# Routed attention and a mixture of experts on one core: similarities and router logits computed transposed, in column tiles of 32

## The chip, the cores and the metric

One core of one Trainium2 chip. The metric is the device time of one execution in microseconds, as the median of the runs shown; lower is better.

## The reference

Attention over 4 batch elements, 8 heads, 768 tokens and a head size of 64, in which a query sees only the keys of its own cluster; then a layer of 8 experts of which each token takes one.

```
q_assign = argmax(einsum('bhsd,hcd->bhsc', q_n, c_n))     # 16 centroids per head
k_assign = argmax(einsum('bhsd,hcd->bhsc', k_n, c_n))
mask     = q_assign[:, :, :, None] == k_assign[:, :, None, :]
attn     = softmax(where(mask, q @ k.T / 8, -1e9))
x        = (attn @ v)  ->  (3072 tokens, 512)
logits   = x @ w_gate                                     # 8 experts
e, gate  = argmax(logits), softmax(logits)[argmax]
out      = gate * (relu(x @ w1[e]) @ w2[e])               # 512 -> 1024 -> 512
```

All inputs and outputs are fp32. An argmax takes the first of equal values.

## The kernel before

The work has three stages. The first is attention with the router's logits. Two heads of one batch element make a group; there are 16 groups, four for each batch element. The rows of q and k are turned by the tensor engine (`turn`, three pieces), so that `qk[g]` has the 2 x 64 components of two heads on the partitions and the tokens along the free dimension. `similar(g)` multiplies each block of 128 tokens, as the stationary operand, with the 32 centroids of the two heads (`cblk`, block diagonal), for q and k: 12 matmuls, whose result already has the tokens on the partitions. `assign` and `assign2` make a one-hot row of each token's cluster on VectorE and GpSimd (`ohs`), `put(g, 0)` for q and `put(g, 1)` for k turn the one-hot rows to `ohT`. A masked score is then a second matmul of `ohT` added on top of the first of `qk`, and the exponential of ScalarE (`A`) makes the masked ones zero. `score(u)` does this for one block of 128 keys against 384 queries of both heads, `attend(u)` multiplies with v two blocks later (the two heads in two column tiles of 64), `T` adds up the denominators on VectorE, and `finish(g, half)` sums them over the partitions, takes the reciprocal on VectorE and writes the normalized half into `XT[b, hp]`.

When the four groups of a batch element are done, `x_turn(b, j)` turns `XT` back into rows, `logits` multiplies each block of 128 tokens of `XT`, stationary, with `wg` (8 columns), accumulated over four blocks of 128 components, `gate` makes the gate's value, and `keep_rows` writes the rows to a DRAM buffer.

The order is written out by hand. One group has 12 units u; the loop takes two units at a time, and one such iteration issues the two scores, two attends, and then the jobs that `at(u, ...)` placed at these units. The jobs of a group g lie around the units of the group before it (LEAD = 14, LAG = 2). Counted from the first unit of the group before: turn at -2 to 0, finish of the last group's second half at 2, similar at 2, assign at 3, assign2 at 5, put 0 at 7, finish of this group's first half at 8, put 1 at 8. For a batch element, counted the same way in the group that follows it, x_turn stands at 3 to 8, logits at 4 and 6, gate at 8, keep_rows at 9.

PSUM has three pools: two tiles of two banks for scores, two for the attended sums, and `ps_m`, two tiles named `mps`, for everything else: turn, similar, put, finish, x_turn and logits take turns in these two. A tile is free when the instruction that reads it out is done; which of the two a job gets is fixed when the kernel is built.

The second stage is the routing: from the logits `lg` VectorE works out for each token its expert and its place in the expert's list, and matmuls scatter the token numbers into index tables. The third stage gathers the rows of each expert by indirect DMA, runs the two layers, and scatters the results. Its weights are loaded three experts ahead. The function `in_general` is a way out for inputs that would overflow and doesn't run here.

Of the kernel before, what the change touches and what calls it, by code (L numbers as in the profile page):

```python
# [8 lines left out]
F32 = mybir.dt.float32  # L9
# [4 lines left out]
ALU = mybir.AluOpType  # L14
# [168 lines left out]
def kernel(  # L183
# [11 lines left out]
    nc = tc.nc  # L195
    B, H, S, D = q.shape
    C = centroids.shape[1]
    P = 128
    NQ = S // P
    HP = H // 2  # L200
    NG = B * HP
    HS = S // 2
    G = 4 * NQ
    N = B * S
    Dm = H * D
    E = moe_w_gate.shape[1]
    F = moe_w1.shape[2]
    DB = Dm // P
    FB = F // P
    NT = N // P  # L210
    KA = D + C
    XW = Dm + 4
    assert D == 64 and H * C == P and NQ * P == S and DB * P == Dm and FB * P == F

    NJ = N // E // P
    CAP = NJ * P
# [6 lines left out]
    consts = ctx.enter_context(tc.tile_pool(name="consts", bufs=1))  # L223
# [3 lines left out]
    def fetch(e):  # L227
        w1 = wpool.tile([P, DB, F], F32, name="w1")
        w2 = wpool.tile([P, FB, Dm], F32, name="w2")
        nc.sync.dma_start(out=w1, in_=moe_w1[bass.ds(e, 1)].rearrange("e (a p) f -> p (e a) f", p=P))  # L230
        nc.sync.dma_start(out=w2, in_=moe_w2[bass.ds(e, 1)].rearrange("e (a p) d -> p (e a) d", p=P))
        return w1, w2
# [3 lines left out]
    ident = consts.tile([P, P], F32)  # L236
    ident_b = consts.tile([P, P], BF16)

    def iota(name, shape, pattern, base, mult):
        ti = consts.tile(shape, I32, name=name + "_i")  # L240
        tf = consts.tile(shape, F32, name=name)
        nc.gpsimd.iota(ti, pattern=pattern, base=base, channel_multiplier=mult)
        nc.gpsimd.tensor_copy(tf, ti)
        return tf

    lg = rte.tile([P, NT, E], F32)
# [6 lines left out]
    with ExitStack() as actx:  # L253
# [3 lines left out]
        asg = actx.enter_context(tc.tile_pool(name="asg", bufs=2))  # L257
        ap = actx.enter_context(tc.tile_pool(name="ap", bufs=4))
        tp_ = actx.enter_context(tc.tile_pool(name="tsum", bufs=2))
        stat = actx.enter_context(tc.tile_pool(name="stat", bufs=2))  # L260
# [4 lines left out]
        ps_m = actx.enter_context(tc.tile_pool(name="ps_m", bufs=2, space=PSUM))  # L265
# [4 lines left out]
        def load(g):  # L270
            b, hp = divmod(g, HP)
            for name, src in (("q", q), ("k", k)):
                t = rows[g, name] = ld.tile([P, NQ, 2, D], F32, name=name + "_in")
                for a in range(2):
                    nc.sync.dma_start(out=t[:, :, a, :], in_=src[b, 2 * hp + a].rearrange("(p j) d -> p j d", j=NQ))
            t = rows[g, "v"] = ld.tile([P, 2, NQ, D], F32, name="v_in", bufs=3)
            nc.sync.dma_start(
                out=t.rearrange("p a j d -> p a (j d)"),
                in_=v[b, 2 * hp : 2 * hp + 2].rearrange("a (p j) d -> p a (j d)", j=NQ),
            )  # L280

        csb = consts.tile([P, D], F32)
        nc.scalar.dma_start(out=csb, in_=centroids.rearrange("h c d -> (h c) d"))
        wg = consts.tile([P, DB, E], F32)
        nc.scalar.dma_start(out=wg, in_=moe_w_gate.rearrange("(a p) e -> p a e", p=P))
        load(0)
        load(1)
        make_identity(nc, ident)
# [1 line left out]
        first_c = iota("first_c", [P, C], [[-1, C]], C, 0)  # L290
        first_e = iota("first_e", [P, E], [[-1, E]], E, 0)
        ones_h = consts.tile([P, D], F32)
        nc.gpsimd.memset(ones_h, 1.0)
        nc.gpsimd.memset(rsum, 0.0)
        nc.gpsimd.memset(rlow, 0.0)

        ohs = []
        for i in range(2):
            t = consts.tile([P, 2 * NQ, 2, D], BF16, name=f"oh{i}")
# [23 lines left out]
        cblk = consts.tile([P, HP, 2, C], F32)  # L323
# [6 lines left out]
        qk, sims, ohT = {}, {}, {}  # L330
# [20 lines left out]
                nc.scalar.copy(dst, src)  # L351

        def similar(g):
            ps = ps_m.tile([P, 512], F32, name="mps")
            for w in range(2):
                for j in range(NQ):
                    c0 = (w * NQ + j) * 2 * C
                    nc.tensor.matmul(  # L358
                        ps[:, c0 : c0 + 2 * C], lhsT=qk[g][:, w, j * P : (j + 1) * P],
                        rhs=cblk[:, g % HP].rearrange("p a c -> p (a c)"), start=True, stop=True,  # L360
                    )
            sims[g] = asg.tile([P, G, C], F32, name="sim")
            nc.scalar.copy(sims[g], ps[:, 0 : G * C].rearrange("p (t c) -> p t c", c=C))

        def assign(g):

            sim = sims.pop(g)
            mx = asg.tile([P, G], F32, name="mx")
            nc.vector.tensor_reduce(mx, sim, axis=AX, op=ALU.max)
            rank = asg.tile([P, G, C], F32, name="rank")  # L370
            nc.vector.tensor_tensor(rank, sim, mx.unsqueeze(2).to_broadcast([P, G, C]), op=ALU.is_ge)
            nc.gpsimd.tensor_tensor(rank, rank, first_c[:, None, :].to_broadcast([P, G, C]), op=ALU.mult)
            sims[g] = rank

        def assign2(g):
            rank = sims.pop(g)
# [7 lines left out]
        def put(g, w):  # L384
            if w == 0:
                ohT[g] = ohp.tile([P, 2, S], BF16, name="ohT")
            ps = ps_m.tile([P, 512], F32, name="mps").bitcast(BF16)
            for j in range(NQ):
                nc.tensor.transpose(
                    ps[:, j * P : (j + 1) * P], ohs[g % 2][:, w * NQ + j].rearrange("p a c -> p (a c)"), ident_b  # L390
                )
            if w == 0:
                nc.scalar.copy(ohT[g][:, 0, :], ps[:, 0:S])
            else:
                nc.vector.tensor_scalar(
                    ohT[g][:, 1, :], ps[:, 0:S], scalar1=BIG, scalar2=-BIG, op0=ALU.mult, op1=ALU.add
                )
# [3 lines left out]
        X, XT = {}, {}  # L401
# [63 lines left out]
                nc.tensor.transpose(ps[:, c * P : (c + 1) * P], XT[b, c][:, j * P : (j + 1) * P], ident)  # L465
            nc.scalar.copy(X[b][:, j, 0:Dm], ps)

        def logits(b, js):
            ps = ps_m.tile([P, 512], F32, name="mps")
            for i, j in enumerate(js):  # L470
                for c in range(DB):
                    nc.tensor.matmul(
                        ps[:, i * E : (i + 1) * E], lhsT=XT[b, c][:, j * P : (j + 1) * P], rhs=wg[:, c, :],
                        start=(c == 0), stop=(c == DB - 1),
                    )
            nc.vector.tensor_copy(
                lg[:, b * NQ + js[0] : b * NQ + js[-1] + 1, :],
                ps[:, 0 : len(js) * E].rearrange("p (j e) -> p j e", e=E),
            )

        def gate(b):
            ts = slice(b * NQ, (b + 1) * NQ)
# [19 lines left out]
        def at(u, f, *a):  # L502
            jobs.setdefault(u, []).append((f, a))
# [3 lines left out]
        for g in range(NG):  # L507
            u0 = g * UG - LEAD
            for piece in range(3):
                at(u0 + piece, turn, g, piece)  # L510
            at(u0 + 4, similar, g)
            at(u0 + 5, assign, g)
            at(u0 + 7, assign2, g)
            at(u0 + 9, put, g, 0)
            at(u0 + 10, put, g, 1)
            for half in range(2):
                at(g * UG + (half + 1) * NQ + LAG, finish, g, half)
        for g in range(2, NG):
            at((g - 2) * UG + LAG + 2, load, g)
        for b in range(B):  # L520
            u0 = (b + 1) * HP * UG + LAG + 1
            for j in range(NQ):
                at(u0 + j, x_turn, b, j)
            at(u0 + 1, logits, b, (0, 1, 2))
            at(u0 + 3, logits, b, (3, 4, 5))
            at(u0 + 5, gate, b)
            at(u0 + 6, keep_rows, b)

        def early(e):
# [40 lines left out]
    with tc.tile_pool(name="sm", bufs=1) as sm, tc.tile_pool(name="rps", bufs=1, space=PSUM) as rps:  # L570
# [23 lines left out]
            op=ALU.is_gt,  # L594
# [11 lines left out]
            op=ALU.is_le,  # L606
# [75 lines left out]
    mps = mctx.enter_context(tc.tile_pool(name="moe_ps", bufs=3, space=PSUM))  # L682
# [77 lines left out]
    with tc.If(nx > XU):  # L760
        with tc.For_i(XU, nx, 1) as i:
# [4 lines left out]
            g = dict(n=1, w=fetch(ex), gi=lambda j: gi[:, 0:1], si=lambda j: gi[:, 1:2], apart=False)  # L766
# [35 lines left out]
```

## Time and profile before

| | us |
|---|---|
| median of 3 runs | 1006.79 |
| lowest, highest run | 993.57, 1011.89 |
| profiled execution, its own time | 1008.31 |
| its span, first to last instruction | 1006.5 |
| attention stage, from the first score to the last attend | 20.3 to 499 |
| tail of the logits and routing, to the first matmul of the experts | 499 to 547.6 |
| experts | 547.6 to 1006.5 |

The mean granted clock of the tensor engine over the span is 0.934 of full speed (2.4 GHz); it has two levels, 1.00 and 0.50 (1.2 GHz), and a mean between them says how long each held.

An fp32 matmul stands in the trace as two passes, each with its own weight load; so 12 matmuls of `similar` are 24 rows of MATMUL and 24 of LDWEIGHTS. PE is the matmul, PEld the weight load. Matmul ends are modelled, so the length of a block is better read from the start of one block to the start of the next. The bracket at the end of a timeline row is the idle time of that engine before it and what released it.

### The profile page before, as it was taken

How to read it: one execution, taken by the hardware profiler on the slowest of the kernel's cores; microseconds unless marked ns; L12 is line 12 of the kernel's file. 1: busy time of each engine (PE TensorE's matmuls, PEld its weight loads, DVE VectorE, ACT ScalarE, POOL GpSimd, SP SyncE). 2: the span in 40 equal slices, each digit the busy share in tenths (PEclk: the TensorE clock that was granted, in tenths of full speed). 3: DMA queues.
4: the chain of work that ended last, by engine and by line, in shares of the span. 5: the costliest groups of instructions: out<-in, count | busy, mean ns of one | idle time of the engine just before them, and what ended most of it. 6: DMA issues, size and time to landing. Idle time of an engine off the chain costs nothing. (4 is left out here: it accounts for less than half of the span.)

```text
span 1006.5 us, 11290 instructions
## 1 busy us (share of the span) xinstructions
PE 941.5 (94%) x4655; PEld 525.4 (52%) x4655; DVE 386.2 (38%) x493; ACT 257.1 (26%) x392; POOL 210.8 (21%) x218
## 2 busy tenths in 40 slices
PE   5999999999999999999967999999999999988896
PEld 4555555454555555555365555545455454555664
DVE  2677745677447775477752101011010100000110
ACT  4444434444334443344410010101100010010100
POOL 3133321333113332132323020101201011010100
PEclk8999989999789998899955999999999999998998
DMA  7016223161221612100012242324334233446610
GB/s 166 16 41 214 49 48 109 32 199 35 48 80 32 215 48 48 73 7 1 1 63 64 83 145 97 133 105 160 141 128 146 100 131 125 159 165 223 236 62 9
DMA packets 82587, 99.02 MB, mean 98 GB/s; under 512 B 52959, under 2 KB 57055, under 8 KB 82016
## 3 DMA queue, kind: packets, MB, share of 16 engines
q1 hardware_dynamic: 76480, 77.60, 24.9%
q0 software_dynamic: 5376, 20.56, 5.2%
q8 instruction: 39, 0.64, 0.3%
q14 instruction: 20, 0.16, 0.1%
q10 hardware_dynamic: 672, 0.05, 0.0%
HBM read 85.57 MB, written 14.20 MB: 99 GB/s over the span
## 5 line engine op out<-in xcount | busy, mean ns | idle before, releaser
L706 PE MATMUL hp<-xgT,w 128*128 128x384 f32 (+1 forms) x896 | 212.9, 399 | 0.8 <-DVE xgT L698 0.8
L719 PE MATMUL zp<-w,h_sb 128*128 128x512 f32 x480 | 211.2, 599 | 0.0
L419 ACT ACTIVATE A<-sps 128x768 f32<-128x768 f32 x192 | 155.2, 811 | 110.9 <-PE sps L417 106.7
L414 PE MATMUL sps<-qk 64*128 64x384 f32 x768 | 183.1, 557 | 0.4 <-ACT A L419 0.4
L706 PEld LDWEIGHTS hp<-xgT,w 128*128 128x128 f32 x896 | 142.4, 193 | 74.2 <-issue 8.6
L426 DVE TENSOR_TENSOR T<-T,A 128x768 f32<-128x768 f32 x128 | 133.9, 1046 | 88.8 <-ACT A L419 82.7
L711 DVE TENSOR_SCALAR h_sb<-hp 128x384 f32<-128x384 f32 (+1 forms) x56 | 24.8, 444 | 359.2 <-PE hp L706 359.2
L434 PE MATMUL O<-A,v_in 128*64 128x384 f32 x768 | 149.7, 512 | 0.0
L719 PEld LDWEIGHTS zp<-w,h_sb 128*128 128x128 f32 x480 | 91.4, 193 | 109.8 <-issue 109.8
L725 POOL DMA_INDIRECT out_dram<-zo,s_idx x30 | 30.1, 1002 | 391.5 <-ACT zo L724 378.5
L454 POOL TENSOR_TENSOR rsum<-rsum,rd 128x384 f32<-128x384 f32 x32 | 32.0, 1000 | 333.0 <-DVE rd L450 333.0
L434 PEld LDWEIGHTS O<-A,v_in 128*64 128x64 f32 x768 | 48.4, 141 | 89.0 <-issue 88.9
L414 PEld LDWEIGHTS sps<-qk 64*128 64x128 f32 x768 | 69.6, 203 | 46.9 <-issue 25.6
L450 DVE RECIPROCAL rd<-mps 128x384 f32<-128x384 f32 x32 | 81.8, 2557 | 3.2 <-PE mps L446 2.1
L724 ACT ACTIVATE zo<-zp,xg 128x512 f32<-128x512 f32 x30 | 20.6, 687 | 222.1 <-PE zp L719 222.1
L713 ACT ACTIVATE h_sb<-hp 128x384 f32<-128x384 f32 (+1 forms) x56 | 22.3, 399 | 214.8 <-PE hp L706 214.8
L417 PE MATMUL sps<-ohT 64*128 64x384 bf16 x384 | 69.0, 352 | 0.0
L358 PEld LDWEIGHTS mps<-cblk,qk 128*128 128x128 f32 x384 | 44.3, 193 | 9.2 <-issue 9.2
L455 POOL TENSOR_SCALAR rd<-rd 128x384 f32<-128x384 f32 x32 | 45.9, 1433 | 2.8
L422 DVE SCALAR_TENSOR_TENSOR T<-A 128x768 f32<-128x768 f32 x32 | 31.2, 976 | 39.6 <-ACT A L419 39.6
L358 PE MATMUL mps<-cblk,qk 128*128 128x32 f32 x384 | 46.0, 278 | 0.0
L697 PE MATMUL tp<-ident,xg 128*128 128x128 f32 x120 | 19.3, 298 | 21.2 <-DMA xg<-x_rows,g_idx 18.8
(140 smaller groups left out, 556.0 us busy)
## 6 DMA issues: line engine op xcount, KB each, us to landing
w<-in_moe_w_dram SPq DMA_DIRECT2D x28, 2048.0 KB, 9.4
x_rows<-x POOLq DMA_DIRECT2D x4, 1548.0 KB, 5.5
q_in<-in_q_dram SPq DMA_DIRECT2D x32, 192.0 KB, 4.4
k_in<-in_k_dram SPq DMA_DIRECT2D x32, 192.0 KB, 4.7
v_in<-in_v_dram SPq DMA_DIRECT2D x16, 384.0 KB, 3.3
xg<-x_rows,g_idx POOLq DMA_INDIRECT x30, 6.9
out_dram<-zo,s_idx POOLq DMA_INDIRECT x30, 2.7
csb<-in_centroids_dram ACTq DMA_DIRECT2D x1, 32.0 KB, 1.9
```

The lines of the kernel that those rows point to most:

```text
L358: nc.tensor.matmul(ps[:, c0 : c0 + 2 * C], lhsT=qk[g][:, w, j * P : (j + 1) * P], rhs=cblk[:, g % HP].rearrange("p a c -> p (a c)"), start ...
L414: nc.tensor.matmul(ps[:, a, 0:HS], lhsT=qk[g][r, 1, ks], rhs=qk[g][r, 0, qs], start=True, stop=False)
L417: nc.tensor.matmul(ps[:, a, 0:HS], lhsT=ohT[g][r, 1, ks], rhs=ohT[g][r, 0, qs], start=False, stop=True)
L419: nc.scalar.activation(A[u], ps[:, :, 0:HS], AF.Exp)
L422: nc.vector.scalar_tensor_tensor(T[g, half], in0=A[u - 1], scalar=1e-9 / P, in1=A[u], op0=ALU.add, op1=ALU.add)
L426: nc.vector.tensor_tensor(T[g, half], T[g, half], A[u], op=ALU.add)
L434: nc.tensor.matmul(O[g, half][a * D : (a + 1) * D, 0:HS], lhsT=rows[g, "v"][:, a, j, :], rhs=a_[:, a, :], start=(j == 0), stop=(j == NQ - 1),)
L450: nc.vector.reciprocal(rd, ps[:, 0:HS])
L454: nc.gpsimd.tensor_tensor(rsum, rsum, rd, op=ALU.add)
L455: nc.gpsimd.tensor_scalar(rd, rd, scalar1=1e-30, scalar2=None, op0=ALU.is_lt)
L706: nc.tensor.matmul(hp[:, :cols], lhsT=g["w"][0][:, c, fb * P : (fb + 1) * P], rhs=g["xT"][:, c, :cols], start=(c == 0), stop=(c == DB - 1),)
L719: nc.tensor.matmul(zp, lhsT=g["h"][:, fb, j * P : (j + 1) * P], rhs=g["w"][1][:, fb, :], start=(fb == 0), stop=(fb == FB - 1),)
```

## The change

`similar` makes the centroids the stationary operand, 32 columns, and moves the tokens: four matmuls (q and k, two halves of 384 tokens each), each into its own 32 partitions of one PSUM tile, that is into its own column tile of the array. The result `simT` is copied by ScalarE and has the centroids on the partitions. A new step `similar2`, two units later, turns it by three transposes into the form that `assign` wants, with a second copy by ScalarE; the order of the token blocks in it is another, which `put` undoes by its index. `assign` works in place.

`logits` does the same with `wg`, padded from 8 to 32 columns (GpSimd clears it and copies the 8 columns in), in three column tiles of 256 tokens for a whole batch element at once; `logits2` turns the result by two transposes and VectorE copies it into `lg`.

The order changes with it: similar2 at 4, assign at 5 (before 3), assign2 at 6 (5), put 0 at 8 (7), put 1 at 9 (8); logits at 3, one block in place of two at 4 and 6, logits2 at 5, gate at 7 (8).

```diff
--- before.py
+++ after.py
@@ -210,7 +210,7 @@
     NT = N // P
     KA = D + C
     XW = Dm + 4
-    assert D == 64 and H * C == P and NQ * P == S and DB * P == Dm and FB * P == F
+    assert D == 64 and C == 16 and H * C == P and NQ % 2 == 0 and NQ * P == S and DB * P == Dm and FB * P == F
 
     NJ = N // E // P
     CAP = NJ * P
@@ -281,8 +281,8 @@
 
         csb = consts.tile([P, D], F32)
         nc.scalar.dma_start(out=csb, in_=centroids.rearrange("h c d -> (h c) d"))
-        wg = consts.tile([P, DB, E], F32)
-        nc.scalar.dma_start(out=wg, in_=moe_w_gate.rearrange("(a p) e -> p a e", p=P))
+        wg_in = consts.tile([P, DB, E], F32)
+        nc.scalar.dma_start(out=wg_in, in_=moe_w_gate.rearrange("(a p) e -> p a e", p=P))
         load(0)
         load(1)
         make_identity(nc, ident)
@@ -291,6 +291,9 @@
         first_e = iota("first_e", [P, E], [[-1, E]], E, 0)
         ones_h = consts.tile([P, D], F32)
         nc.gpsimd.memset(ones_h, 1.0)
+        wg = consts.tile([P, DB, 32], F32)
+        nc.gpsimd.memset(wg, 0.0)
+        nc.gpsimd.tensor_copy(wg[:, :, 0:E], wg_in)
         nc.gpsimd.memset(rsum, 0.0)
         nc.gpsimd.memset(rlow, 0.0)
 
@@ -351,26 +354,33 @@
                 nc.scalar.copy(dst, src)
 
         def similar(g):
+
             ps = ps_m.tile([P, 512], F32, name="mps")
-            for w in range(2):
-                for j in range(NQ):
-                    c0 = (w * NQ + j) * 2 * C
-                    nc.tensor.matmul(
-                        ps[:, c0 : c0 + 2 * C], lhsT=qk[g][:, w, j * P : (j + 1) * P],
-                        rhs=cblk[:, g % HP].rearrange("p a c -> p (a c)"), start=True, stop=True,
-                    )
+            for t in range(4):
+                w, half = divmod(t, 2)
+                nc.tensor.matmul(
+                    ps[t * 2 * C : (t + 1) * 2 * C, 0:HS], lhsT=cblk[:, g % HP].rearrange("p a c -> p (a c)"),
+                    rhs=qk[g][:, w, half * HS : (half + 1) * HS], start=True, stop=True,
+                )
+            sims[g] = asg.tile([P, HS], F32, name="simT", bufs=1)
+            nc.scalar.copy(sims[g], ps[:, 0:HS])
+
+        def similar2(g):
+            simT = sims.pop(g)
+            ps = ps_m.tile([P, 512], F32, name="mps")
+            for i in range(NQ // 2):
+                nc.tensor.transpose(ps[:, i * P : (i + 1) * P], simT[:, i * P : (i + 1) * P], ident)
             sims[g] = asg.tile([P, G, C], F32, name="sim")
-            nc.scalar.copy(sims[g], ps[:, 0 : G * C].rearrange("p (t c) -> p t c", c=C))
+            nc.scalar.copy(sims[g], ps[:, 0:HS].rearrange("p (t c) -> p t c", c=C))
 
         def assign(g):
 
             sim = sims.pop(g)
             mx = asg.tile([P, G], F32, name="mx")
             nc.vector.tensor_reduce(mx, sim, axis=AX, op=ALU.max)
-            rank = asg.tile([P, G, C], F32, name="rank")
-            nc.vector.tensor_tensor(rank, sim, mx.unsqueeze(2).to_broadcast([P, G, C]), op=ALU.is_ge)
-            nc.gpsimd.tensor_tensor(rank, rank, first_c[:, None, :].to_broadcast([P, G, C]), op=ALU.mult)
-            sims[g] = rank
+            nc.vector.tensor_tensor(sim, sim, mx.unsqueeze(2).to_broadcast([P, G, C]), op=ALU.is_ge)
+            nc.gpsimd.tensor_tensor(sim, sim, first_c[:, None, :].to_broadcast([P, G, C]), op=ALU.mult)
+            sims[g] = sim
 
         def assign2(g):
             rank = sims.pop(g)
@@ -387,7 +397,7 @@
             ps = ps_m.tile([P, 512], F32, name="mps").bitcast(BF16)
             for j in range(NQ):
                 nc.tensor.transpose(
-                    ps[:, j * P : (j + 1) * P], ohs[g % 2][:, w * NQ + j].rearrange("p a c -> p (a c)"), ident_b
+                    ps[:, j * P : (j + 1) * P], ohs[g % 2][:, (j % (NQ // 2)) * 4 + w * 2 + j // (NQ // 2)].rearrange("p a c -> p (a c)"), ident_b
                 )
             if w == 0:
                 nc.scalar.copy(ohT[g][:, 0, :], ps[:, 0:S])
@@ -465,18 +475,32 @@
                 nc.tensor.transpose(ps[:, c * P : (c + 1) * P], XT[b, c][:, j * P : (j + 1) * P], ident)
             nc.scalar.copy(X[b][:, j, 0:Dm], ps)
 
-        def logits(b, js):
+        lgTs = {}
+
+        def logits(b):
+
             ps = ps_m.tile([P, 512], F32, name="mps")
-            for i, j in enumerate(js):
-                for c in range(DB):
+            w = S // 3
+            for c in range(DB):
+                for t in range(3):
                     nc.tensor.matmul(
-                        ps[:, i * E : (i + 1) * E], lhsT=XT[b, c][:, j * P : (j + 1) * P], rhs=wg[:, c, :],
+                        ps[t * 32 : (t + 1) * 32, 0:w], lhsT=wg[:, c, :], rhs=XT[b, c][:, t * w : (t + 1) * w],
                         start=(c == 0), stop=(c == DB - 1),
                     )
-            nc.vector.tensor_copy(
-                lg[:, b * NQ + js[0] : b * NQ + js[-1] + 1, :],
-                ps[:, 0 : len(js) * E].rearrange("p (j e) -> p j e", e=E),
-            )
+            lgTs[b] = stat.tile([96, w], F32, name="lgT", bufs=1)
+            nc.scalar.copy(lgTs[b], ps[0:96, 0:w])
+
+        def logits2(b):
+            lgT = lgTs.pop(b)
+            w = S // 3
+            ps = ps_m.tile([P, 512], F32, name="mps")
+            for i in range(w // P):
+                nc.tensor.transpose(ps[:, i * 96 : (i + 1) * 96], lgT[:, i * P : (i + 1) * P], ident[0:96, 0:96])
+            for i in range(w // P):
+                nc.vector.tensor_copy(
+                    lg.rearrange("p (b t i) e -> p b t i e", b=B, t=3)[:, b, :, i, :],
+                    ps[:, i * 96 : (i + 1) * 96].rearrange("p (t e) -> p t e", t=3)[:, :, 0:E],
+                )
 
         def gate(b):
             ts = slice(b * NQ, (b + 1) * NQ)
@@ -509,10 +533,11 @@
             for piece in range(3):
                 at(u0 + piece, turn, g, piece)
             at(u0 + 4, similar, g)
-            at(u0 + 5, assign, g)
-            at(u0 + 7, assign2, g)
-            at(u0 + 9, put, g, 0)
-            at(u0 + 10, put, g, 1)
+            at(u0 + 6, similar2, g)
+            at(u0 + 7, assign, g)
+            at(u0 + 8, assign2, g)
+            at(u0 + 10, put, g, 0)
+            at(u0 + 11, put, g, 1)
             for half in range(2):
                 at(g * UG + (half + 1) * NQ + LAG, finish, g, half)
         for g in range(2, NG):
@@ -521,9 +546,9 @@
             u0 = (b + 1) * HP * UG + LAG + 1
             for j in range(NQ):
                 at(u0 + j, x_turn, b, j)
-            at(u0 + 1, logits, b, (0, 1, 2))
-            at(u0 + 3, logits, b, (3, 4, 5))
-            at(u0 + 5, gate, b)
+            at(u0, logits, b)
+            at(u0 + 2, logits2, b)
+            at(u0 + 4, gate, b)
             at(u0 + 6, keep_rows, b)
 
         def early(e):

```

## Rows read from the trace of the kernel before

**Rows 1.** The page, busy time of each engine over the span: us, share, instructions.
```profile
PE 941.5 (94%) x4655; PEld 525.4 (52%) x4655; DVE 386.2 (38%) x493; ACT 257.1 (26%) x392; POOL 210.8 (21%) x218
```

**Rows 2.** Table by stage: window, length, busy us per engine (instructions), TensorE clock, DMA.
```profile
20.30:499.00 478.70, 467.77 (x2973) 244.25 (x2972) 314.36 (x331) 204.84 (x289) 132.39 (x113) 0.93 0.24 69
499.00:547.60 48.60, 30.09 (x142) 27.32 (x142) 22.82 (x62) 3.65 (x7) 16.81 (x17) 0.56 0.18 61
547.60:1006.50 458.90, 434.19 (x1484) 245.76 (x1484) 42.85 (x83) 42.95 (x86) 53.40 (x54) 0.98 0.37 129
```

**Rows 3.** Timeline of one steady group: start, us, engine, line, operation [idle before].
```profile
106.66 2.87 PE L358 MATMUL mps<-cblk,qk 128*128 128x32 f32 x24
106.78 2.56 DVE L450 RECIPROCAL rd<-mps 128x384 f32<-128x384 f32 x1
...
109.46 0.92 PE L414 MATMUL sps<-qk 64*128 64x384 f32 x4
109.57 0.48 ACT L363 COPY sim<-mps 128x384 f32<-128x384 f32 x1 [4.07 <-PE mps L358]
...
111.28 1.51 PE L434 MATMUL O<-A,v_in 128*64 128x384 f32 x8
...
112.72 0.92 PE L414 MATMUL sps<-qk 64*128 64x384 f32 x4
...
116.14 0.51 PE L389 MATMUL mps<-ident_b,oh 128*128 128x128 bf16 x6
...
116.58 0.92 PE L414 MATMUL sps<-qk 64*128 64x384 f32 x4
116.69 0.80 ACT L393 COPY ohT<-mps 128x768 bf16<-128x768 bf16 x1 [1.24 <-PE mps L389]
```

**Rows 4.** Timelines of PE: a short stretch of attention, one of experts.
```profile
100.73 0.54 PE L434 MATMUL O<-A,v_in 128*64 128x384 f32 x2
...
599.83 6.62 PE L706 MATMUL hp<-xgT,w 128*128 128x384 f32 x20
```

**Rows 5.** Timeline of PE where x_turn and logits of the first batch element run.
```profile
136.38 1.11 PE L465 MATMUL mps<-ident,xT 128*128 128x128 f32 x4 [0.57 <-ACT sim L363]
...
142.30 2.74 PE L472 MATMUL mps<-wg,xT 128*128 128x8 f32 x24
...
159.09 0.51 PE L389 MATMUL mps<-ident_b,oh 128*128 128x128 bf16 x6
...
161.82 0.66 PE L465 MATMUL mps<-ident,xT 128*128 128x128 f32 x4 [2.22 <-DVE rd L450]
...
162.40 0.92 PE L414 MATMUL sps<-qk 64*128 64x384 f32 x4
```

**Rows 6.** Table between similarity blocks: window, length, PE busy, clock, DMA.
```profile
78.87:106.66 27.79, 27.79 (x178) 0.94 0.59 181
106.66:132.95 26.29, 26.19 (x179) 1.00 0.20 48
...
256.26:303.60 47.34, 44.00 (x251) 0.78 0.19 59
```

**Rows 7.** The same table behind a similarity block, and behind x_turn's wait.
```profile
81.70:85.00 3.30, 3.30 (x13) 0.50 1.02 384
...
162.00:165.40 3.40, 3.40 (x24) 1.00 0.02 5
```

**Rows 8.** Timeline of the tail: last finish, last copy of logits.
```profile
500.33 0.87 PE L446 MATMUL mps<-T,ones_h 128*64 128x384 f32 x4 [1.41 <-DVE T L426]
...
515.06 0.18 DVE L476 COPY lg<-mps 128x24 f32<-128x24 f32 x1 [5.31 <-PE mps L472]
```

**Rows 9.** Timeline of the start; the load of w_gate: KB, landing.
```profile
1.22 0.45 ACTq L285 DMA_DIRECT2D wg<-in_moe_w_gate_dram  x1
...
2.42 0.41 POOL L294 MEMSET rsum<- 128x384 f32 x1
...
wg<-in_moe_w_gate_dram ACTq DMA_DIRECT2D x1, 16.0 KB, 3.3
```

## The prediction

> **What bounds the kernel now.** I read the page's busy times first, then a table of busy time by stage, then the timeline of one steady group, then the same table cut at the groups' borders, last the timelines of the tail and the start. TensorE (PE) is busy 94% of the span [rows 1]. By stage [rows 2] it is busy 468 of 479 us in attention, while VectorE (DVE) has 314 us there and ScalarE (ACT) 205; the routing stage between has 49 us at a mean granted clock of 0.56; the experts' stage is PE again and holds nothing that the diff touches. So in attention a microsecond of PE is a microsecond of the kernel, as long as DVE (314/16 = 20 us of 30 per group) stays below it; in routing the chain over DVE and PE counts.
>
> The timeline shows what PE does for the similarities [rows 3]: 24 passes (two for each fp32 matmul) of 128 stationary and 32 moving columns start at 106.66, and the next block starts at 109.46. The block costs **2.80 us**, 0.117 a pass, though a pass moves only 32 columns: it goes at the pace of its weight loads. The logits do the same with 8 columns, 24 passes in 2.74 us [rows 5].
>
> The groups' borders show a second cost. A group takes 26.29 us where the granted clock is 1.00 and 27.79 where it is 0.94 [rows 6], and right after a similarity block PE stands at the lower level, 1.2 GHz (clock 0.50) [rows 7]. One of these drops costs 1.5 us; the clock lost in that group is 0.06 x 27.8 = 1.67 us, so 0.9 of lost clock becomes time. In the whole attention stage 0.07 x 479 = 33 us of clock are lost [rows 2]; with the rounding of 0.93, some 29 us of time. The group whose border runs through x_turn and logits is the worst: clock 0.78 over 47.34 us [rows 6].
>
> **The change, part by part.** Durations are of the profiled execution, 1008.31 us (span 1006.5, and 1.8 around it); the median of the three runs is 1006.79, so nothing has to be moved from one to the other.
>
> *similar.* Now four tiles of 32 stationary columns, each 384 columns moving in two passes. A 384-column fp32 pass alone takes 0.32 us (20 of them in 6.62 us with the last one's end) [rows 4]. Two 64-column tiles run side by side: two passes begin within the same tenth of a microsecond [rows 4], and eight passes with the change of tile shape behind them take 112.72 - 111.28 = 1.44 us [rows 3], which is 4 x 0.32 + 0.16. Four at once is not in this trace. Bounds: all four together 2 x 0.32 + 0.16 = 0.80 us; two together 1.44; one after another 8 x 0.32 + 0.16 = 2.72. I take 0.80, because the nearest row has as many side by side as there are tiles. Saved: 2.80 - 0.80 = 2.00 us a group.
>
> The Trainium skill (TensorE: Matmul & The Clock Gate, Part 3, the table of measured speedups) has three column tiles at 2.38 times, not 3. At that efficiency the four-tile passes take 0.82 us for 0.64 and the three-tile logits 2.15 for 1.70; the estimate for the whole would be 4.5 us higher. The row with two tiles shows no such loss, and no run here shows four.
>
> *similar2.* Three transposes. Four with their change of shape take 162.40 - 161.82 = 0.58 us [rows 5]; three of four are 0.44 us. Its input is copied a whole iteration earlier, so PE doesn't wait for it, and its copy on ACT (0.48 us in the old place) falls into ACT's free half.
>
> *put moves.* Before, put(g,0) and put(g,1) stand in two iterations, the second behind finish. Now both stand behind finish(.,0), and with finish they need three buffers of ps_m, which has two. put 0 gets the other one; put 1 has to wait either for put 0's copy on ACT or for finish's reciprocal on DVE. The copy ends at 116.69 + 0.80, that is 1.35 us after the first transpose at 116.14, and the block alone takes 0.44 [rows 3]: a stall of 0.91, with release 0.95. The reciprocal is seen in its full size where x_turn waits for it behind one put: 2.22 us [rows 5]. Which buffer is taken is fixed when the kernel is built; x_turn at 136.38 took the one that ACT frees, not the one of the reciprocal [rows 5], and ACT is the earlier here too, so I take 0.95; the other end is 2.22. One change of shape (0.16) goes away, as the two puts stand together. Behind the stalled put stand the next scores, so all of it is lost. The longer chain from similar2 over DVE, GpSimd (POOL) and DVE to put has two iterations of 3.3 us and more; I cost it at nothing, and if rank came late it would show as up to 1 us before put 0. DVE has 20 us in a group of now 25.5, so it doesn't become the bound.
>
> A group without x_turn: -2.80 + 0.80 + 0.44 + 0.95 - 0.16 = **-0.77 us, 12 times: -9.2**.
>
> *logits.* For each batch element two blocks of 2.7 us become 24 passes of 256 columns, 0.213 us each by the 384-column row; three together 8 x 0.213 + 0.16 = 1.86 (one by one 5.3, which is the old price), and 0.3 for the two transposes. But they move up into the iteration of the last finish, and need its second half of xT and a third buffer. From the end of finish: reciprocal 0.12 later and 2.56 long [rows 3], then xT. PE fills this with similar (0.8), the wait of x_turn for simT's copy that is there today (0.57 [rows 5]) and x_turn (0.58); it then waits some 0.8 us for a buffer. The last of the four accumulation steps comes due after xT is there. One iteration later four blocks share the two buffers: 0.35 us of waits. In the put iteration today's 159.09 to 162.40 [rows 5] with its 2.22 wait becomes put 0, wait, x_turn, wait, put 1, some 3.0 us, while the earlier put's 0.44 goes. Sum for such a group: -2.00 + 0.44 - 5.40 + 1.86 + 0.3 + 1.15 - 0.8 = **-4.5, 3 times: -13.4**.
>
> *Tail.* Nothing overlaps the last batch element: 14.7 us from the finish at 500.33 to the copy of the logits at 515.06 [rows 8]. Two blocks at 1.2 GHz and one x_turn between go ahead of it no more; 8 to 9 us leave, 2.5 to 3 come back. What is late next are the x_turns that now stand behind. **-6** (from -3 to -8).
>
> *Start.* GpSimd now copies w_gate behind its load: issued at 1.22 and 3.3 to land, so some 4.5 to 4.9, while GpSimd is there at 2.4 [rows 9]. All that follows, cblk's clearing too, comes 2.3 us later, of which 0.9 or so is slack before DVE needs it. **+1.5** (0 to 2.5).
>
> *Clock.* If the narrow blocks are what drops it, most of the 29 us return. The new blocks stream wide columns. What stays narrow is put, stall, put (1.8 us), and it is shorter than the block and wait of 3.3 us after which the clock stays at 1.00 [rows 7]. I take four fifths: **-23**; the ends are 0 and -29.
>
> Sum: -9.2 - 13.4 - 6 + 1.5 - 23 = -50, so 1008.3 - 50 = **958 us**.
>
> **The rivals.**
> (a) *put 1 gets the reciprocal's buffer.* 1.27 us more in each of 15 groups, 19 us, and a hole long enough that some of the clock is lost again, say 4: 981. For it: exactly this wait is in the trace at x_turn. Against: where ACT frees earlier, its buffer was taken. The Trainium skill (TensorEngine Tiling, PSUM Bottleneck) warns of this kind: with tiling the copies out of PSUM may become the limit. As a mechanism of this kernel this is the wait for the two ps_m buffers, and its time is this 981.
> (b) *The clock does not come back,* because transposes and stalls take the place of the narrow blocks: 958 + 23 = 981. For: put and similar2 are narrow too. Against: the stretch at 162 stays at 1.00 after the longest such hole.
> (c) *The column tiles go two at a time:* 0.64 x 15 + 0.85 x 4 = 13 more, 971.
> (d) *The change doesn't do what it says: one tile at a time.* 1.92 x 15 + 3.4 x 4 = 42 more: 1000, no change. **Slower** it gets by the same mechanism if a stream that fills 32 of 128 columns drops the clock as the present block does: the 23 don't return, and 1023 or more follows. It decides from a block of 0.80 + 50/15 = 4.1 us on; eight passes one by one at 1.2 GHz are 5.1. Against: two tiles demonstrably overlap.
>
> **How the numbers follow.** Forecast 0.55, (a) 0.15, (b) 0.12, (c) 0.08, (d) 0.10, half of it slower. The forecast's own range is 942 to 970. To hold 8 in 10 I go from 940 (all of the clock back, no put stall) to 985, which takes in (a), (b) and (c). 2% of the time is 20 us, about what this kernel's runs can tell from no change (they span 18). Under 987 lie the forecast, (c) and most of (a) and (b): faster 0.84; same 0.11, from (d) and from (a) with (b) together; slower 0.05.
>
> **What would show it.** Right: the similarity block takes about 0.8 us with its eight passes starting in two lots of four; put's second lot starts 1.4 us after the first and waits for ACT; groups last 25.5 us at a clock of 1.00 and nearly all are alike; attention's mean clock is at least 0.98; the logits are copied some 9 us after the last finish; the experts' stage keeps its 459 us. Wrong: passes of similar starting 0.32 us apart, a wait of 2.2 us for the reciprocal in every group, or drops to 0.50 behind put or behind the new logits.

## The result

The changed kernel takes 948.13 us (median of 4 runs, 947.51 to 950.44) against 1005.37 before (4 runs, 993.57 to 1011.89): ratio 0.9472, 95% interval 0.9388 to 0.9556. The forecast was 958 in 940 to 985. The profiled execution took 948.49, its span is 946.8. Lines move by 25 or less: similar is L361 now, similar2 L372, put L399, score L424 and L427, attend L444, finish L456 to L466, x_turn L475, logits L486, logits2 L498 and L500.

The page and the table by stage, as [rows 1, 2]:

```profile
PE 871.0 (92%) x4359; PEld 453.9 (48%) x4359; DVE 391.2 (41%) x493; ACT 266.2 (28%) x412; POOL 207.5 (22%) x220
```

```profile
21.64:448.80 427.16, 407.20 (x2712) 185.77 (x2711) 317.57 (x331) 213.18 (x307) 128.71 (x113) 1.00 0.27 77
448.80:489.10 40.30, 22.93 (x122) 17.51 (x120) 22.74 (x62) 3.93 (x8) 16.81 (x17) 0.63 0.22 74
489.10:946.80 457.70, 432.57 (x1484) 245.12 (x1484) 42.88 (x83) 42.95 (x86) 53.39 (x54) 0.98 0.36 130
```

Attention went from 478.7 us at a mean clock of 0.93 to 427.2 at 1.00. A steady group, to be laid beside [rows 3]:

```profile
104.39 0.85 PE L361 MATMUL mps<-qk,cblk 128*32 128x384 f32 x8
104.51 2.56 DVE L460 RECIPROCAL rd<-mps 128x384 f32<-128x384 f32 x1
105.17 0.92 PE L424 MATMUL sps<-qk 64*128 64x384 f32 x4
...
108.43 0.55 PE L372 MATMUL mps<-ident,simT 128*128 128x128 f32 x3
108.91 0.92 PE L424 MATMUL sps<-qk 64*128 64x384 f32 x4
...
116.07 0.51 PE L399 MATMUL mps<-ident_b,oh 128*128 128x128 bf16 x6
...
116.61 0.80 ACT L403 COPY ohT<-mps 128x768 bf16<-128x768 bf16 x1 [1.71 <-PE mps L399]
117.46 0.50 PE L399 MATMUL mps<-ident_b,oh 128*128 128x128 bf16 x6 [0.89 <-ACT ohT L403]
117.89 0.92 PE L424 MATMUL sps<-qk 64*128 64x384 f32 x4
```

The similarity block costs 105.17 - 104.39 = 0.78 us where it was 2.80, similar2 0.48, and the two puts 117.89 - 116.07 = 1.82, with a wait of 0.89 for ACT's copy of put 0. All four tiles run at once: within 0.07 us four passes have begun (timeline of PE from 104.38 to 104.45; the other four follow 0.35 us later):

```profile
104.39 0.53 PE L361 MATMUL mps<-qk,cblk 128*32 128x384 f32 x4
```

The table between similarity blocks, as [rows 6]:

```profile
53.35:78.87 25.52, 24.63 (x165) 1.00 0.22 61
78.87:104.39 25.52, 24.63 (x165) 1.00 0.66 201
...
129.91:164.79 34.88, 31.86 (x215) 0.95 0.24 78
241.36:274.59 33.23, 30.21 (x215) 1.00 0.26 82
```

All groups without x_turn last 25.5 us at a clock of 1.00. The one drop left in attention (34.88 for 33.23) lies behind the longest new hole, where x_turn and both puts wait for the two ps_m tiles. The same hole stands at all three batch borders (147.97, 259.41 and 369.21), and a drop follows one of them:

```profile
147.97 0.51 PE L399 MATMUL mps<-ident_b,oh 128*128 128x128 bf16 x6
...
149.37 0.66 PE L475 MATMUL mps<-ident,xT 128*128 128x128 f32 x4 [0.89 <-ACT ohT L403]
...
150.70 0.50 PE L399 MATMUL mps<-ident_b,oh 128*128 128x128 bf16 x6 [0.67 <-ACT x L476]
151.12 1.04 PE L424 MATMUL sps<-qk 64*128 64x384 f32 x4
```

The logits run as forecast too, 132.70 to 134.55 = 1.85 us:

```profile
132.70 1.93 PE L486 MATMUL mps<-xT,wg 128*32 128x256 f32 x24 [0.68 <-ACT x L476]
134.55 0.92 PE L424 MATMUL sps<-qk 64*128 64x384 f32 x4
```

The tail and the start, as [rows 8, 9]:

```profile
450.12 0.87 PE L456 MATMUL mps<-T,ones_h 128*64 128x384 f32 x4 [1.26 <-DVE T L436]
...
457.76 0.26 DVE L500 COPY lg<-mps 128x24 f32<-128x24 f32 x2
```

```profile
4.48 0.21 POOL L296 COPY wg<-wg_in 128x32 f32<-128x32 f32 x1 [1.62 <-DMA wg_in<-in_moe_w_gate_dram]
...
7.98 0.20 POOL L327 MEMSET cblk<- 128x128 f32 x1
```

From the last finish to the logits' copy 7.6 us are left of 14.7. At the start GpSimd waits 1.62 us for the load of w_gate, and the first score comes at 21.64 for 20.3.

### The profile page after: what moved, and what is told of

Read it like the earlier page. It is cut to its first block, busy times and chain, and to the rows that moved or that the text cites. A ratio compares the mean times of both kernels' runs of the same rounds, so it can differ in the third digit from the quotient of the medians.

```text
span 946.8 us, 10723 instructions
## 1 busy us (share of the span) xinstructions
PE 871.0 (92%) x4359; PEld 453.9 (48%) x4359; DVE 391.2 (41%) x493; ACT 266.2 (28%) x412; POOL 207.5 (22%) x220
## 4 chain that ended last, share of the span: by engine, by line
issue 43%; POOL 5%; PE 1%; DVE 1%; POOLq 0%
POOL out_dram L750 3%; POOL xg L712 3%; PE tok_ps L691 1%; POOL oh_c L683 0%; POOLq L750 0%; DVE sl L662 0%; POOLq L783 0%; DVE oh_c L679 0%; PE cps L611 0%; DVE slot L660 0%; DVE slot L659 0%; DVE og L617 0%; DVE slot L658 0%; POOLq L712 0%; DVE slot L654 0%
## 5 line engine op out<-in xcount | busy, mean ns | idle before, releaser
L736 DVE TENSOR_SCALAR h_sb<-hp 128x384 f32<-128x384 f32 (+1 forms) x56 | 24.9, 444 | 357.6 <-PE hp L731 357.6
L424 PE MATMUL sps<-qk 64*128 64x384 f32 x768 | 166.5, 511 | 0.3 <-ACT A L429 0.3
L444 PE MATMUL O<-A,v_in 128*64 128x384 f32 x768 | 145.4, 500 | 0.0
L424 PEld LDWEIGHTS sps<-qk 64*128 64x128 f32 x768 | 63.7, 187 | 50.8 <-issue 26.4
L444 PEld LDWEIGHTS O<-A,v_in 128*64 128x64 f32 x768 | 46.8, 136 | 80.9 <-issue 75.5
L427 PE MATMUL sps<-ohT 64*128 64x384 bf16 x384 | 63.6, 325 | 0.0
L432 DVE SCALAR_TENSOR_TENSOR T<-A 128x768 f32<-128x768 f32 x32 | 39.5, 1233 | 46.8 <-ACT A L429 46.8
L465 POOL TENSOR_SCALAR rd<-rd 128x384 f32<-128x384 f32 x32 | 52.9, 1654 | 2.8
L723 DVE COPY xgT<-tp 128x512 f32<-128x512 f32 x30 | 20.1, 689 | 47.2 <-PE tp L722 47.2
L712 POOL DMA_INDIRECT xg<-x_rows,g_idx x30 | 29.1, 971 | 16.4 <-issue 8.8
```

The source lines that it names most:

```text
L424: nc.tensor.matmul(ps[:, a, 0:HS], lhsT=qk[g][r, 1, ks], rhs=qk[g][r, 0, qs], start=True, stop=False)
L427: nc.tensor.matmul(ps[:, a, 0:HS], lhsT=ohT[g][r, 1, ks], rhs=ohT[g][r, 0, qs], start=False, stop=True)
L432: nc.vector.scalar_tensor_tensor(T[g, half], in0=A[u - 1], scalar=1e-9 / P, in1=A[u], op0=ALU.add, op1=ALU.add)
L444: nc.tensor.matmul(O[g, half][a * D : (a + 1) * D, 0:HS], lhsT=rows[g, "v"][:, a, j, :], rhs=a_[:, a, :], start=(j == 0), stop=(j == NQ - 1),)
L465: nc.gpsimd.tensor_scalar(rd, rd, scalar1=1e-30, scalar2=None, op0=ALU.is_lt)
L712: nc.gpsimd.indirect_dma_start(out=g["xg"][:, j, :], out_offset=None, in_=x_d[:, :], in_offset=bass.IndirectOffsetOnAxis(ap=g["gi"](j), ax ...
```

## The experiments

What was to be told apart is the larger half of the gain, the clock, and the price of the puts. Each run is compared with the kernel before on the same chip. Where the time moves by about 1% or less, the argument rests on the granted clock in the one profiled execution of the run. A drop counts as behind a block if the clock falls to 0.50 within 5 us of the block's start; in the kernel before these are 10 of the 15 similarity blocks after the first. The kernel before scatters by itself: its runs beside the ones with added work go from 995.72 us at a mean clock of 0.946 to 1010.33 us at 0.936.

**Half blocks.** Nothing is taken away; similar is cut in two.

```diff
-        def similar(g):
+        def similar(g, w):
             ps = ps_m.tile([P, 512], F32, name="mps")
-            for w in range(2):
...
-            at(u0 + 4, similar, g)
+            at(u0 + 2, similar, g, 0)
+            at(u0 + 4, similar, g, 1)
```

> The kernel before, with nothing taken away: the 12 similarity matmuls of a group are cut into the q half and the k half, two units apart (k where all twelve stood), each with its own PSUM tile and copy. Theory N (a long block of narrow passes is what drops the clock): no drop to 0.50 behind the similarity blocks any more; groups without x_turn all last 26.3 + 0.16 = 26.5 us at a clock of 1.00; drops behind the logits stay; the whole is 8 to 13 us faster than before, about 995. Rival R (the clock came back because less work was left, or its drops have another cause): drops as before, groups of 26.5 and 28, about 1008.

1004.54 us against 1009.79, ratio 0.9931 (0.9897 to 0.9965). Table from one second half to the next:

```profile
53.30:80.70 27.40, 26.10 (x178) 1.00 0.18 62
80.70:108.11 27.41, 26.11 (x178) 1.00 0.61 178
```

No drop follows any of the 30 half blocks of the steady part; the drops that are left lie at the batch borders, where the logits stayed. That is what theory N expects, with no work taken away, so it doesn't take less work to bring the clock back, as rival R has it. The run alone doesn't prove N, for its groups are also spaced otherwise, and the runs below show drops vanish with whole blocks too. What speaks for N is all the runs together: every one with whole blocks has drops behind some of them (10, 5, 3, 3, 1 and 6 of 15), and the five without, with groups of 24.9 to 27.4 us, have none there.

The time was forecast too low, for a group lasts 27.4, not 26.5: put 0 now waits 1.31 us for the one-hot rows. The similarities are copied by 109.99, but VectorE takes them up only at 111.30, when it is done with finish's reciprocal and xT. From there over GpSimd to put the chain had no slack, and the q half is no longer among the work of TensorE beside it:

```profile
108.23 2.56 DVE L453 RECIPROCAL rd<-mps 128x384 f32<-128x384 f32 x1
...
109.67 0.32 ACT L363 COPY sim<-mps 128x192 f32<-128x192 f32 x1 [2.73 <-PE mps L357]
...
111.30 0.54 DVE L372 TENSOR_REDUCE mx<-sim 128x24 f32<-128x384 f32 x1
...
117.46 0.51 PE L392 MATMUL mps<-ident_b,oh 128*128 128x128 bf16 x6 [1.31 <-DVE oh L382]
```

**The two parts alone.** The diffs are the parts of the change's own diff.

> The change without its logits: similar, similar2 and the new place of put as in the kernel after, logits and gate as before. By the sum: -0.77 us in each of 15 groups (-11.5) and, by theory N, the clock behind the similarity blocks (some 11 drops of 1.5, -16): 977. Drops remain behind the logits alone. By rival R, which gives this part only its work: 993.

964.77, ratio 0.9549 (0.9527 to 0.9571). Its groups last 25.5 us at a clock of 1.00, as in the whole change; in attention only 10 us at 1.2 GHz are left, behind the logits. The time lies 12 us below the forecast by theory N.

> The change without its similarities: logits and logits2 as in the kernel after, similar and put as before, assign in place to make room for the new tile. By the sum: about -3.8 us at each of three batch borders (-11), -7 in the tail, +1.4 at the start, and by theory N some 8 drops behind the logits, -12: 976. Groups without x_turn stay as they were, 26.3 or 27.8 with a drop behind similar. By rival R 988. The savings of this run and of the one without the new logits should add up to that of the whole change, 57.

981.12, ratio 0.9706 (0.9676 to 0.9735), 5 us above the forecast by theory N. Groups are 26.28, or 27.76 with a drop:

```profile
56.66:84.42 27.76, 27.76 (x179) 0.94 0.20 54
...
112.18:138.46 26.28, 26.18 (x178) 1.00 0.20 47
178.97:205.26 26.29, 26.19 (x179) 1.00 0.21 57
```

No drop begins behind the new logits. But two of the three old holes with a wait of 2.22 us at put and x_turn are followed by one here (after 164.71 and after 284.11), though the same hole was followed by none in the three cases of before. The savings of the two parts, 45.0 and 28.7, make 73.7 us, more than the 61.7 that the whole change is below the 1009.79 of these runs (57.2 below its own runs of before): the forecast that they add up failed. In each run the part that was left as it was has fewer drops too. Behind the old logits 10 us at 1.2 GHz are left of 27, and behind the old similarities 5 drops of 10, though the groups keep their 26.28 us. From the first score to the last finish 64.9 us stood at 1.2 GHz before, 12.2 and 30.7 stand there in the two parts, 3.9 in the whole. At 1.2 GHz half of the clock is lost, and by the prediction's 0.9 of lost clock that becomes time, the parts saved 24 and 15 us of it and the whole 27.5, and the 12 us too many are drops that both parts take away. So the clock's share isn't a sum of fixed prices for each block.

**The place of the puts,** alone, on the kernel before:

```diff
-            at(u0 + 9, put, g, 0)
-            at(u0 + 10, put, g, 1)
+            at(u0 + 10, put, g, 0)
+            at(u0 + 11, put, g, 1)
```

> The kernel before with only the places of put 0 and put 1 as in the kernel after (both behind finish); similar, assign and logits stay where they were. By the sum the two ps_m tiles cost 0.95 us a group here too, less one change of tile shape: groups at a clock of 1.00 last 26.28 + 0.95 - 0.16 = 27.1 us, with a wait of 0.9 for the copy of put 0 before the second lot of transposes; the whole is some 10 us slower than before on equal clock. Rival: before, the chain from similar over assign to put 0 had no slack (put 0 waited 0.17 us for it), so that put 0's later place gives back what the wait takes and groups stay at 26.3 to 26.5.

The groups did as forecast: 27.06 us, with the wait of 0.89 for put 0's copy. The whole did the opposite: 994.93 against 1009.04, ratio 0.9879 (0.9829 to 0.9929), faster with a longer group. Of the 15 similarity blocks, unchanged, 3 are followed by a drop, where 10 were before:

```profile
53.34:80.40 27.06, 26.17 (x178) 1.00 0.19 54
...
173.97:202.68 28.71, 27.82 (x179) 0.94 0.19 54
```

Theory N thus needed a second half: a narrow block can drop the clock, and something else decides which one does.

**Work that nobody uses,** to see whether that is where a block falls in time, or the order of the puts. Between similar and put 0 of the kernel before (shown with 384 columns; the other two runs have 192 columns, and two matmuls of 384):

```diff
+        def fill(g):
+            ps = ps_m.tile([P, 512], F32, name="mps")
+            for i in range(1):
+                nc.tensor.matmul(ps[:, 0:384], lhsT=ident, rhs=qk[g][:, i, 0:384], start=(i == 0), stop=(i == 0))
...
+            at(u0 + 6, fill, g)
```

> The kernel before with added work that nobody uses: between similar and put 0 of each group one fp32 matmul with 128 stationary and 192 moving columns, 0.32 + 0.16 = 0.48 us of TensorE. Nothing else moves. On equal clock a group lasts 26.76 and the whole is 7 us longer, 1016. Theory S (which of the narrow blocks drops the clock hangs on where in time it falls, so on the spacing of the groups): the number of drops behind the 15 similarity blocks differs from the 10 of before, and the time with it, by 1.5 us for each. Theory O (the order of put took the drops away in the run with puts together): about 10 of 15 stay, 1016.

> The same with 384 moving columns: 0.64 + 0.16 = 0.80 us a group, so that groups at a clock of 1.00 last 27.1 us as in the run with the puts together (27.06), with put's order left as it was. Theory S: as few drops as there (2 to 4 of 15) and a whole of 995 to 1000, faster than before in spite of 12 us more work. Theory O: about 10 of 15 drops and 1021.

> The same with two such matmuls: 1.28 + 0.16 = 1.44 us a group, 27.7 us at a clock of 1.00. On equal clock 22 us longer than before, 1031. Theory S: again another number of drops, from none (1010) to nearly all (1035). Theory O: 10 of 15, 1031.

All three against 1008.53: 999.58 (0.9929, 0.9874 to 0.9985), 999.59 (0.9940, 0.9906 to 0.9975), 1015.09 (1.0077, 1.0048 to 1.0106). Groups at a clock of 1.00 last 26.64, 26.96 and 27.61 us, 0.35, 0.67 and 1.32 more than before and about 0.1 less than forecast; drops follow 3, 1 and 6 of the 15 similarity blocks. The run with 384 columns:

```profile
56.37:84.98 28.61, 28.61 (x181) 0.94 0.20 54
84.98:111.94 26.96, 26.96 (x181) 1.00 0.62 191
```

In 15 groups the added work makes 5, 10 and 20 us. The first two made the kernel 9 us faster, the third 7 slower: from the first score to the last finish 27.3, 23.9 and 37.6 us stand at 1.2 GHz, where 64.9 did before. The order of put isn't needed for it, so theory O fell. Nor is it the amount of wide work, for the most has more drops than the middle one, and the run with the puts together had 3 with none added. Theory S asked for little, for two of the runs only another number than 10, for the third 2 to 4 drops (1 came) and 995 to 1000 us (999.59). It holds as far as that: small shifts of time change the number. The spacing of the groups doesn't fix it alone, for the run with the new logits had 5 at 26.28 us where the kernel before had 10, and each count is of one execution.

**Put 0 ahead of finish,** on the changed kernel:

```diff
-                at(g * UG + (half + 1) * NQ + LAG, finish, g, half)
+                at(g * UG + (half + 1) * NQ + LAG + 1 - half, finish, g, half)
```

> The kernel after with put 0 moved ahead of finish for the first half (finish one unit later), so that finish fills the time in which put 1 waits for the copy of put 0 out of the second ps_m tile. If that wait is a loss of TensorE time as costed (0.95 us a group): the wait of 0.89 before L399 falls to about 0.2, a group lasts 24.8 in place of 25.5, 11 us in all: 937. Rival: the wait was cover for VectorE, which is late afterwards, and a group keeps 25.5: 947.

936.01, ratio to before 0.9263 (0.9238 to 0.9288), 12 us below the 948.13 of the changed kernel:

```profile
113.73 0.51 PE L399 MATMUL mps<-ident_b,oh 128*128 128x128 bf16 x6
114.17 0.87 PE L456 MATMUL mps<-T,ones_h 128*64 128x384 f32 x4
114.27 0.80 ACT L403 COPY ohT<-mps 128x768 bf16<-128x768 bf16 x1 [1.07 <-PE mps L399]
...
115.12 0.49 PE L399 MATMUL mps<-ident_b,oh 128*128 128x128 bf16 x6
115.55 0.92 PE L424 MATMUL sps<-qk 64*128 64x384 f32 x4
```

The copy now runs while finish's passes do, and the wait is nearly gone: 115.55 - 113.73 = 1.82 us hold both puts and finish. Groups last 24.88 us, and the clock stays at 1.00 in all of attention. It was a loss of TensorE time.

**The padding of w_gate later,** on top of that:

```diff
-        wg = consts.tile([P, DB, 32], F32)
-        nc.gpsimd.memset(wg, 0.0)
-        nc.gpsimd.tensor_copy(wg[:, :, 0:E], wg_in)
...
         nc.gpsimd.memset(cblk, 0.0)
+        wg = consts.tile([P, DB, 32], F32)
+        nc.gpsimd.memset(wg, 0.0)
+        nc.gpsimd.tensor_copy(wg[:, :, 0:E], wg_in)
```

> The kernel with put 0 ahead of finish (936 us), and GpSimd's padding of w_gate moved behind the clearing of cblk, so that nothing waits behind the load of w_gate. If the start is 1.4 us later because of that wait: the first exponential comes 1.4 us earlier, at some 22.5 us, and the whole is 1.4 us faster, 934.6. Rival: the start hangs on the q and k loads or on the clock of the first 20 us, and nothing changes: 936.

The first exponential came at 22.39 us for 23.94, so the start did hang on that wait. In the time, 935.64 (0.9290, 0.9255 to 0.9325) on another chip, the 1.5 us can't be told from nothing. This is the fastest version of the study together with the one above.

## Why the prediction was right

**The mechanism** held step by step. Similar was costed at 0.80 us and took 0.78; similar2 0.44 and 0.48; the two puts together 1.84 (1.40 to the second lot and its 0.44) and 1.82; logits 1.86 and 1.85; a group without x_turn -0.77, and 26.29 - 25.52 = 0.77 was measured. The choice between the bounds, four tiles at once, put 1 in the tile that ACT frees, proved right in each case, so rivals (a), (c) and (d) fell: no wait for the reciprocal stands before L399, and four passes start together. The loss that the Trainium skill (TensorE: Matmul & The Clock Gate, Part 3) has for three column tiles isn't seen here; the measured 0.78 us with four and 1.85 us with three tiles leave no room for it. At the page's figure the estimate for four tiles is 0.81, not the 0.82 that I gave.

**The sum.** From first score to last finish the time fell from 500.33 - 20.28 = 480.05 us to 450.12 - 21.64 = 428.48, by 51.6, where the terms made 45.6. The groups gave their 9.2. A batch border, taken from 47.34 us at 0.78 [rows 6] to a clock of 1.00 by the same 0.9, is 38.0 us before and 33.2 after: -4.8, three times -14.4, for -13.4. What remains, 51.6 - 9.2 - 14.4 = 28, is the clock, **the term that was mis-sized: -23**. The 27.5 from the time at 1.2 GHz agrees. I kept a fifth of the loss for drops in new places; only one came. The tail gave 7.1 for 6, and its routing another 1.2; the start cost 1.4 for 1.5. The experts' stage was 1.2 us shorter, which the change doesn't touch. -51.6 - 7.1 - 1.2 + 1.4 - 1.2 = -59.7, from 1006.5 to 946.8.

**What was right for a weaker reason** than I gave. I argued that the hole of 3.3 us around x_turn leaves the clock alone, from three cases of one trace. The run with the new logits alone has a drop behind two of three such holes, and the changed kernel one behind its longest hole, a drop behind put, which I had named as a sign of being wrong. Rival (b) is thus not wrong in kind; its place was small. And 28 us for the clock is no fixed price of the narrow blocks: in the kernel before 10 of 15 blocks cost 1.5 us each, and work that lengthens a group by 0.35 us leaves 3 of them. By work alone, at equal clock, the change is worth some 30 us. What decides between a block that drops the clock and one that doesn't these runs leave open.

## What to carry to other kernels

Where few moving columns follow each weight load, read the block from start to start: if it goes at the pace of the loads, make the few columns stationary, in as many column tiles as fit, and pay with a transpose. Count the clock from the rows at either level before and after, and apart from the work, since it can hide a loss or make up a gain that a small shift of timing would have given. A job that is moved behind another which shares its two buffers costs the copy between them; put something that needs neither the copy nor the buffer's result between.

## What the runs showed of the hardware

Four column tiles of 32 take the fp32 passes of four matmuls at the same time: eight passes of 384 columns in 0.78 us with the change of tile shape, where one alone takes 0.32. In a periodic kernel small shifts of time change how often the granted clock drops: with the same 15 similarity blocks in them, one profiled execution each with groups of 26.64, 26.96, 27.06 and 27.61 us had 3, 1, 3 and 6 drops behind them, and two kernels with groups of 26.3 us had 10 and 5. The kernels with groups 0.35 and 0.67 us longer were 0.7 and 0.6% faster than the one without the added work. Behind similarity blocks cut in two, or made of wide passes, no drop was seen.
